# First token chunk of a fused attention and squared-ReLU MLP: who writes the high part of the squared features

## The chip, the cores and the metric

One core of one Trainium2 chip runs the whole program. The metric is the device time of one execution in microseconds (us). Three executions of the kernel before took 881.85, 885.22 and 885.75 us; their median is 885.22 us.

## What is computed

```
scores = q @ k.T / 8, masked by head: heads 0-3 see the last 32 positions,
         heads 4-7 see the positions of equal remainder mod 32
attn   = softmax(scores) @ v                      # 8 batches, 8 heads, 576 x 64
x      = attn as 4608 tokens x 512
h      = max(x @ w_in, 0)                         # 4608 x 2048
out    = (h * h) @ w_out                          # 4608 x 512, float32
```

## The kernel before

The 4608 tokens are worked off in 12 chunks of 384 (`TC`). For each chunk the 2048 hidden features are 16 steps of 128. `up(c, j)` (L462) forms the pre-activations of step `j` in a PSUM bank `h`, 128 x 384: every float32 operand is held as a high part, rounded to a shorter format, and a low part, the rest, and a product is the three matmuls high x high, high x low and low x high, so `up` has 12 matmuls of 384 columns. The three banks for `h` are used in turn, so step `j + 3` can start only when the last reader of step `j` is done. The squared ReLU is then split the same way into `gh` (high) and `gl` (the rest), and `down(c, j)` (L489) multiplies them with the output weights, 9 matmuls of 512 columns into three PSUM banks `y`. `down` runs two steps behind `up`.

The first chunk (`c == 0`) differs from the others. While it runs, the 16 weight tiles are still being decoded and split, two halves per step: ScalarE scales the raw words (L154) and makes the low bits `z` in a PSUM bank (L166), VectorE joins them (L169), ScalarE rounds the high part `w` (L172), GpSimd subtracts for the low part (L173). From the fourth step on there is one bank for `z`, so the next `z` waits for L169 of the one before. In the same stretch the attention of chunk 1 is computed: local heads in `pe_pair` (scores L319, row minima L324, GpSimd shift L347, exponential L348, GpSimd scaling L353, transposes L359 copied out by L360, product with v L367, then high part `xlh` on ScalarE, L382, and rest `xll` on VectorE, L383), and strided heads in `strided` (GpSimd products L412 and L434, VectorE sums L413 and L435, a softmax in between, L418 to L425, high part `xsh` L445, rest `xsl` on GpSimd L446). GpSimd also splits the first operands of chunk 2's attention (`kx` L218, `qx` L220, `vx` L255).

For the squared ReLU the first chunk uses a spare buffer `p_t` in SBUF: ScalarE writes `r = relu(h)` there (L470), VectorE writes `max(h, 0) * r` back over the bank `h` (L471), ScalarE rounds it into `gh` (L475), and VectorE subtracts, `gl = h - gh` (L476). In the later chunks ScalarE does ReLU, square and rounding (L473 to L475). `last["gh"]` names the ScalarE instruction behind which the two weight halves of the step are placed.

A scheduler that estimates each engine's time line sets the order of instructions on every engine's queue from the program order, so a change to one operation moves others. Each queue is worked off in order.

The text of the change's functions:

Of the kernel before, what the change touches and what calls it, by code (L numbers as in the profile page):

```python
# [11 lines left out]
AF = mybir.ActivationFunctionType  # L12
ALU = mybir.AluOpType
# [36 lines left out]
def f32(ap):  # L50
    return ap.bitcast(F32)
# [35 lines left out]
def attn_moe(ctx: ExitStack, tc, qk_l, v_l, qk_d, v_d, qk_p, v_p, f_s, q_s, k_s, v_s, w_in, w_out, masks, eye, out):  # L87
    nc = tc.nc
# [13 lines left out]
    def psum(i, nm):  # L102

        return ps.tile([P, 512], F32, name=nm, tag=f"ps{i}")
# [17 lines left out]
    last = {}  # L122
# [329 lines left out]
    def up(c, j):  # L452
        x = xt[c]
        p, o = divmod(j, 2)
        ph = psum((c * NFT + j) % 3, f"h{c}_{j}")
        n = 0
        for kt in range(4):
            kind, kk = "ls"[kt // 2], kt % 2
            xh, xl = x[kind, "h"][:, kk, :], x[kind, "l"][:, kk, :]
            wsl = slice(kt * 256 + o * P, kt * 256 + (o + 1) * P)  # L460
            for w, xx in ((wi[p][0], xh), (wi[p][0], xl), (wi[p][1], xh)):
                done = nc.tensor.matmul(ph[:, :TC], w[:, wsl], xx, start=n == 0, stop=n == 11)  # L462
                n += 1
        gh = gpool.tile([P, TC], F32R, name=f"gh{c}_{j}", tag="gh")
        gl = gpool.tile([P, TC], F32R, name=f"gl{c}_{j}", tag="gl")
        g = ph[:, :TC]
        if c == 0:

            r = p_t[j % 2].rearrange("p w q -> p (w q)")
            nc.scalar.activation(r, g, AF.Relu)  # L470
            nc.vector.scalar_tensor_tensor(out=g, in0=g, scalar=0.0, in1=r, op0=ALU.max, op1=ALU.mult)  # L471
        else:
            nc.scalar.activation(g, g, AF.Relu)  # L473
            nc.scalar.activation(g, g, AF.Square)  # L474
        last["gh"] = nc.scalar.copy(gh, g)  # L475
        nc.vector.tensor_sub(gl, g, f32(gh))  # L476
        g_tiles[c, j] = gh, gl
        return done
# [152 lines left out]
    for s in range(NS + 2):  # L631
        c, j = divmod(s, NFT)
        if s < NFT:
            up(c, j)
            if s >= 2:
                last["pe"] = down(*divmod(s - 2, NFT))

        elif s % 2 == 0:
            before, between, rest = plan[j // 2]
            for part, slots, two in (up, (s, s + 1), before), (down, (s - 2, s - 1), between):  # L640
                take(c + 1, two)
                with tc.issue_after(last["pe"].ins):
                    for i in slots:
                        if 0 <= i < NS:
                            last["mm"] = part(*divmod(i, NFT))
                last["pe"] = last["mm"]
            take(c + 1, rest)
# [110 lines left out]
```

## Time and profile before

| what | value |
|---|---|
| time, median of three | 885.22 us (881.85 to 885.75) |
| the profiled execution's own time | 883.18 us |
| its span, first to last instruction | 881.4 us |
| TensorE busy | 868.5 us of the span |
| ScalarE instructions L470 and L475 in the first chunk | 16 each |
| VectorE instructions L471 and L476 in the first chunk | 16 each |

The page gives busy times for TensorE (PE; PEld are its weight loads), VectorE (DVE), ScalarE (ACT) and GpSimd (POOL). The first chunk's matmuls run from about 31 to 114 us of the span, those of chunk 1 begin at 105 us, and the two overlap there because `down` lags. Matmuls are pipelined: a row of x2 in 0.52 us means that the second began 0.17 us after the first.

### The profile page before, as it was taken

The numbers are of one execution on the slowest core, as the hardware profiler recorded it, in microseconds if no ns is written. First come the engines' busy times: TensorE is split into PE (matmuls) and PEld (weight loads), VectorE is DVE, ScalarE is ACT, GpSimd is POOL, SyncE is SP. The second block draws the span as 40 slices with busy tenths as digits, with TensorE's granted clock in tenths as the row PEclk, the third lists the DMA queues.
The fourth block names the chain that finished last, engine by engine and source line by source line (L and its number), as shares of the span: only waits on it lengthen the run. The fifth ranks groups of instructions, "written<-read, shape, count | busy, mean of one in ns | idle before, by whom it ended". The sixth has DMA issues, their size and how long they took to land.

```text
span 881.4 us, 14862 instructions
## 1 busy us (share of the span) xinstructions
PE 868.5 (99%) x4744; PEld 789.6 (90%) x4744; DVE 635.5 (72%) x1892; ACT 572.6 (65%) x1510; POOL 676.8 (77%) x722
## 2 busy tenths in 40 slices
PE   8899999999999999999999999999999999999997
PEld 7788899999999999999999999999999989998996
DVE  4578687788777888878778778778787787883111
ACT  6798776676676666757657747657666665664332
POOL 4698878878978989898988978997898899782000
PEclk9999999999999999999999999999999999999999
DMA  9851631323123123104102302312131121000000
GB/s 356 355 195 63 184 121 42 103 84 113 32 66 112 37 89 103 44 30 127 44 13 80 115 14 74 104 31 74 31 102 57 30 71 61 7 1 10 28 1 36
DMA packets 26798, 71.41 MB, mean 81 GB/s; under 512 B 2976, under 2 KB 8736, under 8 KB 25184
## 3 DMA queue, kind: packets, MB, share of 16 engines
q1 hardware_dynamic: 26432, 70.14, 23.9%
q8 instruction: 37, 0.61, 0.3%
q10 hardware_dynamic: 288, 0.33, 0.1%
q14 instruction: 41, 0.34, 0.1%
HBM read 61.01 MB, written 9.44 MB: 80 GB/s over the span
## 4 chain that ended last, share of the span: by engine, by line
PE 95%; ACT 3%; DVE 1%; POOL 0%; issue 0%; DVEq 0%; POOLq 0%; ACTq 0%
PE h L462 44%; PE y L489 44%; PE s L234 2%; PE o L280 2%; ACT e L345 1%; PE w_ps L586 1%; ACT raw L154 1%; PE b L319 1%; DVE sc L419 0%; ACT z L166 0%; ACT w L172 0%; DVE raw L169 0%; ACT pt L360 0%; PE b L359 0%; DVE xsl L383 0%
## 5 line engine op out<-in xcount | busy, mean ns | idle before, releaser
L489 PE MATMUL y<-w,gh 128*128 128x512 f32 x1152 | 357.1, 391 | 0.8 <-ACT gh L475 0.8
L489 PEld LDWEIGHTS y<-w,gh 128*128 128x128 f32 x1152 | 212.5, 188 | 41.5 <-ACT gh L475 1.4
L462 PE MATMUL h<-xlh,w 128*128 128x384 f32 x768 | 229.6, 339 | 2.1 <-DVE xsl L383 1.6
L462 PE MATMUL h<-xsh,w 128*128 128x384 f32 x768 | 226.2, 335 | 0.0
L489 PE MATMUL y<-w,gl 128*128 128x512 f32 x576 | 224.0, 392 | 0.0
L434 POOL TENSOR_TENSOR pp<-vs,sc 128x448 f32<-128x448 f32 (+10 forms) x192 | 189.8, 1014 | 39.8 <-DVE qs L435 18.2
L412 POOL TENSOR_TENSOR pq<-ks,qs 128x512 f32<-128x512 f32 (+2 forms) x192 | 197.8, 1050 | 17.9 <-DVE sc L413 13.8
L476 DVE TENSOR_TENSOR gl<-h,gh 128x384 fp32r<-128x384 f32 x192 | 105.4, 550 | 84.2 <-ACT gh L475 82.9
L475 ACT CAST gh<-h 128x384 fp32r<-128x384 f32 x192 | 91.4, 477 | 103.0 <-PE y L489 100.0
L473 ACT ACTIVATE h<-h 128x384 f32<-128x384 f32 x176 | 83.0, 472 | 107.8 <-PE h L462 106.2
L413 DVE TENSOR_REDUCE sc<-pq 128x8 f32<-128x512 f32 (+4 forms) x228 | 119.6, 534 | 46.2 <-POOL pq L412 43.9
L462 PEld LDWEIGHTS h<-xlh,w 128*128 128x128 f32 x768 | 142.1, 188 | 5.6 <-DVE xsl L383 1.8
L462 PEld LDWEIGHTS h<-xsh,w 128*128 128x128 f32 x768 | 141.7, 188 | 0.3
L462 PE MATMUL h<-xll,w 128*128 128x384 f32 x384 | 129.3, 337 | 0.0
L435 DVE TENSOR_REDUCE qs<-pp 128x64 f32<-128x448 f32 (+11 forms) x192 | 106.7, 563 | 31.0 <-POOL pp L434 29.5
L489 PEld LDWEIGHTS y<-w,gl 128*128 128x128 f32 x576 | 108.1, 188 | 22.9
L462 PE MATMUL h<-xsl,w 128*128 128x384 f32 x384 | 128.5, 335 | 0.0
L474 ACT ACTIVATE h<-h 128x384 f32<-128x384 f32 x176 | 83.2, 473 | 3.6
L259 DVE STREAM_TRANSPOSE p_t<-e 32x128 f32<-32x128 f32 x240 | 72.3, 301 | 10.4 <-ACT e L248 6.0
L462 PEld LDWEIGHTS h<-xll,w 128*128 128x128 f32 x384 | 72.5, 189 | 2.2
L462 PEld LDWEIGHTS h<-xsl,w 128*128 128x128 f32 x384 | 72.2, 188 | 0.0
L243 ACT ACTIVATE e<-e,nm 96x128 f32<-96x128 f32 x160 | 62.5, 392 | 10.5 <-DVE nm L226 8.8
(97 smaller groups left out, 1077.2 us busy)
## 6 DMA issues: line engine op xcount, KB each, us to landing
qk<-qk_l SPq DMA_DIRECT2D x24, 400.0 KB, 3.2
y<-ysb SPq DMA_DIRECT2D x36, 256.0 KB, 3.7
raw<-w_in SPq DMA_DIRECT2D x7, 1024.0 KB, 11.2
qk<-qk_l SPq DMA_DIRECT2D x16, 416.0 KB, 3.3
vs<-v_s SPq DMA_DIRECT2D x10, 576.0 KB, 4.0
raw<-w_out SPq DMA_DIRECT2D x5, 1024.0 KB, 12.9
v<-v_l SPq DMA_DIRECT2D x40, 128.0 KB, 2.0
ks<-k_s SPq DMA_DIRECT2D x8, 576.0 KB, 3.8
```

The costliest lines, as they stand in the source:

```text
L243: nc.scalar.activation(e[:QC, cut(w)], e[:QC, cut(w)], AF.Exp, bias=nmax[:QC, w : w + 1], scale=-1.0, accum_out=ssum[:QC, w, :1])
L259: nc.vector.transpose(out=pt[STR * k : STR * (k + 1), :, STR * r : STR * (r + 1)], in_=e.rearrange("p (w k) -> p w k", k=KW)[STR * r : STR ...
L412: nc.gpsimd.tensor_mul(pv, kt[:, a : a + m, :], qt[:, i - i0 : i - i0 + 1, :].broadcast_to([P, m, D]))
L413: nc.vector.tensor_reduce(out=sc[:, i - i0, a : a + m], in_=pv, op=ALU.add, axis=AX.X)
L434: nc.gpsimd.tensor_mul(pv, vt[:, a : a + nd, :n], sc[:, il : il + 1, :n].broadcast_to([P, nd, n]))
L435: nc.vector.tensor_reduce(out=ot[:, il, a : a + nd], in_=pv, op=ALU.add, axis=AX.X)
L462: done = nc.tensor.matmul(ph[:, :TC], w[:, wsl], xx, start=n == 0, stop=n == 11)
L473: nc.scalar.activation(g, g, AF.Relu)
L474: nc.scalar.activation(g, g, AF.Square)
L475: last["gh"] = nc.scalar.copy(gh, g)
L476: nc.vector.tensor_sub(gl, g, f32(gh))
L489: done = nc.tensor.matmul(y_ps[c][t], g[:, sl], w[:, wsl], start=j == 0 and k == 0, stop=j == NFT - 1 and k == 2)
```

## The change

In the first chunk the line with VectorE's multiplication becomes a loop that runs it twice on the same operands: once into `gh`, whose type does the rounding, and once over the bank `h`. The rounding on ScalarE stays for the later chunks alone. The diff also adds a second line with the ReLU of the first chunk: it writes the same values to the same buffer again, and it is now the one that `last["gh"]` names.

```diff
             r = p_t[j % 2].rearrange("p w q -> p (w q)")
             nc.scalar.activation(r, g, AF.Relu)
-            nc.vector.scalar_tensor_tensor(out=g, in0=g, scalar=0.0, in1=r, op0=ALU.max, op1=ALU.mult)
+            last["gh"] = nc.scalar.activation(r, g, AF.Relu)
+            for t in (gh, g):
+                nc.vector.scalar_tensor_tensor(out=t, in0=g, scalar=0.0, in1=r, op0=ALU.max, op1=ALU.mult)
         else:
             nc.scalar.activation(g, g, AF.Relu)
             nc.scalar.activation(g, g, AF.Square)
-        last["gh"] = nc.scalar.copy(gh, g)
+            last["gh"] = nc.scalar.copy(gh, g)
         nc.vector.tensor_sub(gl, g, f32(gh))
```

In the changed program the two ReLUs are L470 and L471, the multiplications L473, the subtraction L478, `down` L491.

**Where the order moves, first place.** VectorE at the first steps of the first chunk, before (L413 and L418 belong to the strided attention of batch 2, L169 to the weights):

```order
L413 TENSOR_REDUCE sc_2_694<-pq_2_1_0_699 128x2
L471 SCALAR_TENSOR_TENSOR h_0_531<-h_0_531,p_t_90 128x384
L413 TENSOR_REDUCE sc_2_694<-pq_2_2_0_702 128x3
L471 SCALAR_TENSOR_TENSOR h_1_562<-h_1_562,p_t_91 128x384
L413 TENSOR_REDUCE sc_2_694<-pq_2_3_0_705 128x4
L476 TENSOR_TENSOR gl_0_545<-h_0_531,gh_0_544 128x384
L169 SCALAR_TENSOR_TENSOR raw_267<-raw_267,z_0_551 128x512
```

and VectorE at the same place with the change:

```order
L413 TENSOR_REDUCE sc_2_698<-pq_2_1_0_703 128x2
L413 TENSOR_REDUCE sc_2_698<-pq_2_2_0_706 128x3
L473 SCALAR_TENSOR_TENSOR gh_0_544<-h_0_531,p_t_90 128x384
L473 SCALAR_TENSOR_TENSOR h_0_531<-h_0_531,p_t_90 128x384
L413 TENSOR_REDUCE sc_2_698<-pq_2_3_0_709 128x4
L169 SCALAR_TENSOR_TENSOR raw_267<-raw_267,z_0_552 128x512
L413 TENSOR_REDUCE sc_2_698<-pq_2_4_0_712 128x5
L478 TENSOR_TENSOR gl_0_545<-h_0_531,gh_0_544 128x384
```

One more reduction now stands ahead of the first multiplication, and the subtraction for `gl_0` has the second multiplication, two reductions and a weight join between it and `gh_0`.

**Second place.** TensorE where the first chunk hands over to chunk 1, before (`h_0` and `h_1` are steps 0 and 1 of chunk 1, `y` with `gl_13` is the end of `down` of step 13):

```order
L489 MATMUL y_2_614<-w_6_1218,gl_13_1307 128x512
L462 MATMUL h_0_1397<-xlh_901,w_0_413 128x384
L462 MATMUL h_0_1397<-xll_902,w_0_413 128x384
L462 MATMUL h_0_1397<-xlh_901,w_0_413 128x384 x2
L462 MATMUL h_0_1397<-xll_902,w_0_413 128x384
L462 MATMUL h_0_1397<-xlh_901,w_0_413 128x384
```

and with the change:

```order
L491 MATMUL y_2_617<-w_6_1230,gl_13_1320 128x512
L462 MATMUL h_0_1413<-xlh_908,w_0_413 128x384
L462 MATMUL h_0_1413<-xll_909,w_0_413 128x384
L462 MATMUL h_0_1413<-xlh_908,w_0_413 128x384
L462 MATMUL h_1_1432<-xlh_908,w_0_413 128x384
L462 MATMUL h_1_1432<-xll_909,w_0_413 128x384
L462 MATMUL h_1_1432<-xlh_908,w_0_413 128x384
L367 MATMUL b_1_1_1295<-pt_1_1_693,v_1_1_690 64x96 x8
L462 MATMUL h_0_1413<-xlh_908,w_0_413 128x384
L462 MATMUL h_1_1432<-xlh_908,w_0_413 128x384
L462 MATMUL h_0_1413<-xll_909,w_0_413 128x384
L462 MATMUL h_0_1413<-xlh_908,w_0_413 128x384
```

The product with v for the second pair of local heads (L367), which stood inside step 14 before, now stands inside the first steps of chunk 1, and the matmuls that follow read what is made from it.

**Third place.** ScalarE at the same hand-over with the change, from the ReLU of step 15 to the first operation of chunk 1 (before, L382 of the second pair stood ahead of the ReLU of step 14, with 11 instructions between it and the first operation of chunk 1):

```order
L470 ACTIVATE p_t_91<-h_15_1382 128x384
L166 ACTIVATE z_512_1290<-raw_512_1109 128x512
L172 CAST w_7_1284<-raw_0_1107 128x512
L217 CAST kx_0_1377<-qk_0_1366 128x448
L219 CAST qx_0_1376<-qk_0_1366 128x384
L254 CAST vx_0_1618<-v_0_1367 128x4x64
L471 ACTIVATE p_t_91<-h_15_1382 128x384
L445 CAST xsh_910<-qkvs_3_981 128x2x192
L172 CAST w_7_1284<-raw_512_1109 128x512
L360 COPY pt_1_1_693<-b_1_1_1249 128x384
L382 CAST xlh_908<-b_1_1_1295 128x384
L475 ACTIVATE h_0_1413<-h_0_1413 128x384
```

The copy L360 that the product waits for, and the rounding L382 behind it, are now the last ScalarE work of the first chunk. On GpSimd the rest `xsl` (L446) moves in the same way, from ahead of `kx`, `qx`, `vx` to behind them:

```order
L173 TENSOR_TENSOR w_7_1284<-raw_0_1107,w_7_1284 128x512
L404 MEMSET sc_4_1510 128x108
L412 TENSOR_TENSOR pq_4_0_0_1512<-qkvs_4_1508 128x64
L412 TENSOR_TENSOR pq_4_1_0_1515<-qkvs_4_1508 128x128
L218 TENSOR_TENSOR kx_0_1377<-qk_0_1366,kx_0_1377 128x448
L220 TENSOR_TENSOR qx_0_1376<-qk_0_1366,qx_0_1376 64x384
L255 TENSOR_TENSOR vx_0_1618<-v_0_1367,vx_0_1618 128x4x64
L662 MEMSET p_t_90 128x384
L446 TENSOR_TENSOR xsl_911<-qkvs_3_981,xsh_910 128x2x192
```

Before, L446 stood right ahead of the first of these rows.

## Rows read from the trace of the kernel before

**Rows 1.** Busy time by stretch (us:us, length, engines with instruction counts, granted clock, DMA).
```profile
core 0: us, PE busy (x) PEld busy (x) DVE busy (x) ACT busy (x) POOL busy (x), PEclk, DMA share, GB/s
36.00:106.00 70.00, 68.73 (x381) 59.82 (x380) 53.70 (x139) 61.50 (x116) 60.57 (x66) 1.00 0.44 155
106.00:200.00 94.00, 93.99 (x496) 85.83 (x495) 73.61 (x246) 64.72 (x187) 76.27 (x91) 1.00 0.30 92
200.00:876.00 676.00, 676.00 (x3535) 617.62 (x3534) 490.13 (x1419) 420.15 (x1141) 522.79 (x541) 1.00 0.18 56
```

**Rows 2.** TensorE in order of time (start us, us, count, idle before) at its two waits.
```profile
39.17 1.66 PE L489 MATMUL y<-w,gh 128*128 128x512 f32 x6 [0.79 <-ACT gh L475]
40.66 0.62 PE L489 MATMUL y<-w,gl 128*128 128x512 f32 x2
...
89.56 0.44 PE L462 MATMUL h<-xlh,w 128*128 128x384 f32 x1 [0.48 <-DVE gl L476]
89.84 0.34 PE L462 MATMUL h<-xll,w 128*128 128x384 f32 x1
90.02 0.51 PE L462 MATMUL h<-xlh,w 128*128 128x384 f32 x2
```

**Rows 3.** VectorE groups from 36 to 106 us (busy us, mean ns, idle before).
```profile
L169 DVE SCALAR_TENSOR_TENSOR raw<-raw,z 128x512 uint32<-128x512 uint32 x26 | 17.8, 683 | 5.0 <-ACT z L166 4.6
L471 DVE SCALAR_TENSOR_TENSOR h<-h,p_t 128x384 f32<-128x384 f32 x16 | 9.0, 561 | 4.6 <-ACT p_t L470 4.5
L476 DVE TENSOR_TENSOR gl<-h,gh 128x384 fp32r<-128x384 f32 x14 | 7.6, 551 | 1.7 <-ACT gh L475 1.7
```

**Rows 4.** ScalarE groups from 36 to 106 us.
```profile
L470 ACT ACTIVATE p_t<-h 128x384 f32<-128x384 f32 x16 | 7.7, 492 | 1.8 <-PE h L462 1.8
L475 ACT CAST gh<-h 128x384 fp32r<-128x384 f32 x14 | 6.8, 488 | 2.5 <-DVE h L471 1.8 <-PE y L489 0.6 <-DVE sm L424 0.2
L360 ACT COPY pt<-b 128x384 f32<-128x384 f32 x4 | 1.9, 482 | 0.4 <-PE b L359 0.4
L382 ACT CAST xlh<-b 128x384 fp32r<-128x384 f32 x2 | 1.0, 480 | 0.0
```

**Rows 5.** GpSimd, VectorE and ScalarE in order of time at the first step.
```profile
37.34 1.02 POOL L412 TENSOR_TENSOR pq<-qkvs 128x128 f32<-128x128 f32 x2
...
38.04 0.56 DVE L471 SCALAR_TENSOR_TENSOR h<-h,p_t 128x384 f32<-128x384 f32 x1
38.51 0.34 DVE L413 TENSOR_REDUCE sc<-pq 128x3 f32<-128x192 f32 x1
...
38.63 0.48 ACT L475 CAST gh<-h 128x384 fp32r<-128x384 f32 x1 [1.78 <-DVE h L471]
```

**Rows 6.** GpSimd, then VectorE, around 80 us in order of time.
```profile
79.16 5.15 POOL L173 TENSOR_TENSOR w<-raw,w 128x512 fp32r<-128x512 f32 x4
...
80.47 3.89 DVE L419 TENSOR_TENSOR sc<-sc,mx 128x36 f32<-128x36 f32 x1
```

**Rows 7.** ScalarE, GpSimd, VectorE, TensorE at the hand-over in order of time.
```profile
102.25 0.54 ACT L445 CAST xsh<-qkvs 128x384 fp32r<-128x384 f32 x1
...
105.73 0.67 ACT L172 CAST w<-raw 128x512 fp32r<-128x512 f32 x1
...
102.86 1.02 POOL L446 TENSOR_TENSOR xsl<-qkvs,xsh 128x384 fp32r<-128x384 f32 x1
103.98 1.31 POOL L173 TENSOR_TENSOR w<-raw,w 128x512 fp32r<-128x512 f32 x1
...
108.88 0.73 POOL L255 TENSOR_TENSOR vx<-v,vx 128x256 fp32r<-128x256 f32 x1
...
102.41 0.56 DVE L383 TENSOR_TENSOR xll<-b,xlh 128x384 fp32r<-128x384 f32 x1 [0.84 <-ACT xlh L382]
...
105.14 0.33 PE L462 MATMUL h<-xlh,w 128*128 128x384 f32 x1
110.09 0.62 PE L489 MATMUL y<-w,gh 128*128 128x512 f32 x2
```

**Rows 8.** All instructions of L169: least, median and greatest duration in ns.
```profile
L169 DVE SCALAR_TENSOR_TENSOR raw<-raw,z x32: 671/689/697, 18.6 to 103.4; 128x512 uint32<-128x512 uint32 x32
```

## The prediction

> **What bounds the kernel now.** I read busy time by stretch first. From 106 us to the end TensorE is busy without a hole, 93.99 of 94 us and 676 of 676, while VectorE, ScalarE and GpSimd stay at 81% or under [rows 1]. There an engine that waits costs nothing; only what ends the first chunk earlier or later moves the end. In the first chunk, 36 to 106 us, TensorE is busy 68.73 of 70 us, ScalarE 61.5, VectorE 53.7, GpSimd 60.6 [rows 1]. So I went on to TensorE's own time line there: it waits twice, 0.79 us for the first `gh`, and 0.48 us for a `gl` [rows 2], by the queue's order that of step 10, whose bank step 13 takes over. These 1.27 us are about all that the first chunk can give back, 0.14% of the time. What it can take has no such ceiling, because ScalarE and VectorE work there close behind TensorE.
>
> **What the change does to each engine.** ScalarE: 16 roundings of 0.488 us go, and 16 repeated ReLUs of 0.492 us come [rows 4], so its load stays where it was, +0.1 us. What it loses is a wait: a rounding had to wait for VectorE's product, 1.8 us in all, and all of it once, at the first step [rows 4, 5]; the repeated ReLU needs only what the first one needed. VectorE: the product into SBUF is new to the trace. Its nearest rows are the product into the bank, 0.561 us, and the subtraction into SBUF in the same rounded type, 0.551 us [rows 3]; I take 0.55, the row with the same output, and the larger weight join, 512 columns from PSUM and SBUF into SBUF at 0.683, bounds it from above [rows 3]. Sixteen are 8.8 us, at most 10.9. VectorE's 53.7 busy us become 62.5 of 70, 89%. Its 16.3 idle us cover that as long as they shrink with it: most are waits for ScalarE's `z` and ReLU, 4.6 and 4.5 us [rows 3]. What it costs if that cover is gone is the first rival. GpSimd and the DMA queues get nothing new; GpSimd's order changes at the hand-over (term 3).
>
> **The chain of one step.** Before: ReLU, product, rounding (`gh`), subtraction (`gl`). Now: two ReLUs, product (`gh`), product, subtraction (`gl`). `gh` has three operations as before, 0.49 + 0.49 + 0.55 against 0.49 + 0.56 + 0.49 [rows 3, 4]; `gl` has five instead of four and comes half a us later. In the steady part `down` runs two steps behind `up`, and a step is 12 matmuls at 0.17 us (0.51 for two, 0.34 for one [rows 2]) and 9 at 0.23 (0.62 for two [rows 7]), 4.1 us. So I cost that half us at nothing in steps 1 to 13. It shows at the first step and in what surrounds the last.
>
> **Term 1, the first step.** VectorE's queue is in order, and the third reduction now stands ahead of the product. Its operand was ready at 38.36, the end of GpSimd's second of two [rows 5]; the reduction takes 0.34, and an operation starts some 0.09 before the end of the one ahead (38.04 + 0.56 against 38.51 [rows 5]). So the product starts near 38.65 and `gh` is there at 39.2, where the rounding gave it at 39.11 [rows 5]: +0.1 us. Then `gl_0`: the second product, two reductions of about 0.4 and 0.5 and a weight join stand before it, from start to start 0.47, 0.33, 0.60 and 0.40, so that the subtraction starts at 40.9 and ends at 41.5. TensorE reaches its first `gl` matmul 1.5 us behind its first `gh` matmul [rows 2], at 40.75, so it stands 0.8 us. **Term 1 is +0.9 us**; 0 if the join doesn't hold it up, 1.5 if the join itself waits for its `z`.
>
> **Term 2, the wait at 89.56.** It comes from one VectorE operation: a subtraction of the strided softmax, 128 x 36 elements, stands 3.89 us, from 80.47 to 84.36, beside an unbroken run of four GpSimd subtractions that ends at 84.31 [rows 6]; all that is queued behind it was late, `gl` of step 10 too. With the change it stands behind `gl` of step 11. I take the wait as gone, **-0.6 us** with the slow start of the matmul behind it (0.44 for 0.34 us [rows 2]). Whether the stall then hits another step is a rival.
>
> **Term 3, the hand-over to chunk 1.** Before, `xll` and `xsl` were ready at 103.0 and 103.9 us, over a us ahead of chunk 1's first matmul at 105.14 [rows 7]. Now L360 and L382 end ScalarE's first chunk. From the end of step 15's matmuls ScalarE has nine operations and L360. The same nine (rounding `xsh`, `z`, two roundings of weights, `kx`, `qx`, `vx`, two ReLUs) ran in one piece from 102.25 to 106.40 [rows 7], 4.15 us, and L360 adds 0.4 [rows 4]: 4.55 us. TensorE has in that time 15 `down` matmuls at 0.23 and six of chunk 1 at 0.17, 4.5 us. So L367 just starts in time. But L382, 0.48 [rows 4], and L383, 0.56 [rows 7], now lie between it and what TensorE needs next, with two matmuls, 0.35 us, in between: about 0.8 us with the hand-offs. GpSimd is later still. Behind step 15, ReLU, `z` and a rounding take some 1.6 us until it may subtract; that subtraction to the end of `vx` took 103.98 to 109.61 [rows 7], 5.6 us, and `xsl` now follows with 1.02: 8.2 us. TensorE wants `xsl` after the 4.5 us, L367, eight more matmuls, 1.4 us, and the 0.8: near 7.1. I take **+1.6 us**, nearer to GpSimd's 1.9 than to the 0.8. Bounds: 0, if ScalarE and GpSimd run as far ahead as ScalarE does at the first step, and 4, if they are two to three us behind.
>
> **The sum.** +0.9 - 0.6 + 1.6 = +1.9 us on the profiled execution's 883.18: 885.1. That execution lies 2.0 us under the median of 885.22, and I set the change against the median: 887.1 us. About 0.5%, 4.4 us, is what a measurement of this kernel can tell from no change; the three runs themselves span 3.9 us. So I forecast no change that counts.
>
> **Rivals.** *VectorE becomes the pace of the first chunk.* Its waits are for ScalarE, whose next `z` waits for VectorE's last join: if the two hold each other, none of the 16.3 idle us shrinks and the 8.8 us come on top. The low part of the last weights' first half was ready at 105.29 and first wanted at 110.09 [rows 7], so 4.8 us are free, and TensorE stands for the other 4.0: 885.22 + 1.9 + 4.0 = 891.1, slower. It decides from the point where the last joins, the last at 103.4 before [rows 8], come more than 5 us later. Against it: 89% is not full, and ScalarE's 1.8 us head start. Chance 0.2.
>
> *The stalled subtraction hits harder.* Between `gl` of step 11 and `gh` of step 12 it holds up weight joins too. If its 3.9 us return where TensorE has some 2 us of slack, that is +2 us: 889.1. The row has a small operation wait out the rest of a run of four [rows 6]. The Trainium skill ("SBUF — State Buffer", Who interferes with whom) has a VectorE instruction with two SBUF inputs and a GpSimd one that reads SBUF exclude each other for one whole instruction; by that it would wait for one GpSimd subtraction, 1.3 us, and this rival would cost nothing. The measured stall speaks for the longer price. The new products have one operand in PSUM, as the joins do, and no join took over 0.697 us [rows 8], so the products themselves aren't held. Chance 0.12.
>
> *ScalarE's freedom carries through.* Weights and attention run 1.8 us ahead from the first step on, the hand-over is covered and both waits go: 885.22 - 1.3 = 883.9. It can't give 0.5%. Chance 0.18.
>
> *The change doesn't do what it says.* ScalarE's rounding goes, but the repeated ReLU takes its slot, so only the wait is freed; this is in the sum already.
>
> **Chances and range.** The forecast has 0.5. Low end: the third rival less the runs' scatter, 883.0; high end: the first rival, 891.1, say 891.5. Over 4.4 us slower is reached by most of the first rival and a little of the second: 0.18. No mechanism gives over 4.4 us faster; scatter leaves 0.04. The rest, 0.78, is within 0.5%.
>
> **What would show it.** Right: no wait of TensorE after 115 us; at 40 us one of 0.8 us, now ahead of the first `gl`; none near 89; one to two us in all between L367 and the first `xsl` matmuls near 107; VectorE at 62 busy us in the first chunk, the new products at 0.55. Wrong: a first chunk longer by over 4 us with weights (L172, L173) as releaser, or products into `gh` far from 0.55.

## The result, and the profile after

The changed kernel took 885.94 us, the median of 20 runs (884.58 to 887.51), beside 884.47 us for the kernel before on the same chips (881.85 to 886.27). The ratio is 1.0019, with a 95% interval of 1.0012 to 1.0026: slower by 1.5 us, within the 0.5% that the prediction called no change, and 1.2 us under its 887.1 us. The changed kernel's profiled execution took 886.62 us, its span 884.8 us.

One thing is needed to compare profiles. Each run's record gives its mean granted clock, and the runs here fall in two groups, 0.993 to 0.998 and 0.985 to 0.990; three executions that fall in neither are left out below, one of the kernel before (0.947, 883.44 us), one of x1 (3251 us) and one of w1 (1742 us). The first views show where the second group loses. Busy time by stretch of the profiled execution of the kernel before (columns as in [rows 1]), from 16 to 36 us, while attention and weights are being prepared:

```profile
16.00:28.00 12.00, 8.25 (x109) 5.98 (x109) 6.35 (x22) 9.64 (x22) 8.27 (x10) 1.00 1.01 416
28.00:36.00 8.00, 6.39 (x44) 6.17 (x39) 4.18 (x7) 7.27 (x13) 4.27 (x4) 0.79 1.02 411
```

The same view of the changed kernel, and its first chunk and the rest:

```profile
16.00:28.00 12.00, 10.42 (x85) 8.07 (x86) 6.34 (x21) 8.43 (x18) 7.55 (x9) 0.60 1.02 420
28.00:36.00 8.00, 7.56 (x51) 6.61 (x50) 3.65 (x6) 7.21 (x12) 3.40 (x3) 0.54 1.01 407
36.00:106.00 70.00, 68.59 (x371) 60.25 (x370) 59.69 (x153) 62.78 (x118) 60.14 (x65) 1.00 0.44 152
106.00:200.00 94.00, 92.88 (x499) 84.32 (x498) 71.70 (x240) 63.18 (x181) 74.76 (x90) 1.00 0.31 94
200.00:876.00 676.00, 676.00 (x3538) 617.79 (x3537) 492.67 (x1427) 422.32 (x1147) 525.95 (x544) 1.00 0.18 56
```

Here TensorE was at its lower level (1.2 GHz) for most of 16 to 36 us, in the profiled execution before only briefly behind 28 us. The two programs have the same TensorE work in that stretch, and yet the last `up` matmul ahead of the first `down` began at 38.04 us before and at 39.82 us after. So 1.8 of the 3.4 us between the two spans lie ahead of the change, 1.45 between there and the last matmul, and 0.2 behind it. Of the 89 runs of the kernel before in these groups, 34 were in the lower one, and on the mean 1.8 us longer (885.12 against 883.35 us). Compared group with group, the change costs **+2.0 us** (11 runs at the higher clock, 885.36 us) and **+1.8 us** (9 runs at the lower, 886.88 us). The forecast was +1.9. The 89 runs come from the four chips of the experiments; against runs of their own chip alone, the versions in the table below move by up to 0.3 us in the higher group and 0.7 in the lower. For the 20 runs of the kernel before beside the changed kernel there are no clocks.

From 200 us on nothing changed, TensorE is busy without a hole as in [rows 1]. From 106 to 200 us it lost 1.1 us. Its time line in the changed kernel, at the five places where it starts late (idle before in brackets):

```profile
40.99 1.66 PE L491 MATMUL y<-w,gh 128*128 128x512 f32 x6 [0.83 <-DVE gh L473]
43.23 0.97 PE L491 MATMUL y<-w,gl 128*128 128x512 f32 x3 [0.58 <-DVE gl L478]
...
107.38 0.88 PE L367 MATMUL b<-pt,v 128*64 128x96 f32 x16 [0.31 <-ACT pt L360]
108.84 0.62 PE L462 MATMUL h<-xlh,w 128*128 128x384 f32 x2 [0.58 <-ACT xlh L382]
...
110.98 0.44 PE L462 MATMUL h<-xsl,w 128*128 128x384 f32 x1 [0.23 <-POOL xsl L446]
```

The first row was there before as 0.79 us [rows 2]; the wait near 89 us of [rows 2] is gone; the other four are new. The bracket is less than what is lost, because the matmul behind a hole starts up slowly. Counted from start to start, and less the usual step, they are 1.00, 0.75, 0.48, 0.77 and 0.40 us, 3.4 us in all; before, 0.95 and 0.66, 1.6 us in all. That is 1.8 us more; from the 38.04 (39.82) matmul to the last matmul of the program it took 1.45 us longer. The 0.35 us between the two counts are not explained.

### The profile page after: what moved, and what is told of

Its sections match the earlier page's. It is cut to its first block, busy times and chain, and to the rows that moved or that the text cites. A ratio compares the mean times of both kernels' runs of the same rounds, so it can differ in the third digit from the quotient of the medians.

```text
span 884.8 us, 14867 instructions
## 1 busy us (share of the span) xinstructions
PE 873.3 (99%) x4744; PEld 793.2 (90%) x4744; DVE 642.2 (73%) x1908; ACT 573.7 (65%) x1510; POOL 677.2 (77%) x722
## 4 chain that ended last, share of the span: by engine, by line
PE 93%; DMA 2%; ACT 2%; POOL 2%; DVE 1%; issue 0%; DVEq 0%; SPq 0%; POOLq 0%; ACTq 0%
PE h L462 44%; PE y L491 43%; PE s L234 2%; PE o L280 2%; DMA raw<-w_in 1%; POOL w L173 1%; ACT raw L154 1%; DMA qk<-qk_d 1%; DMA raw<-w_out 1%; PE b L319 0%; ACT w L172 0%; PE b L359 0%; ACT z L166 0%; PE b L378 0%; PE b L367 0%
## 5 line engine op out<-in xcount | busy, mean ns | idle before, releaser
L491 PE MATMUL y<-w,gh 128*128 128x512 f32 x1152 | 356.7, 391 | 0.8 <-DVE gh L473 0.8
L491 PEld LDWEIGHTS y<-w,gh 128*128 128x128 f32 x1152 | 212.5, 188 | 40.9 <-DVE gh L473 1.1
L491 PE MATMUL y<-w,gl 128*128 128x512 f32 x576 | 224.0, 392 | 0.6 <-DVE gl L478 0.6
L478 DVE TENSOR_TENSOR gl<-h,gh 128x384 fp32r<-128x384 f32 x192 | 105.4, 549 | 83.1 <-ACT gh L477 81.7
L413 DVE TENSOR_REDUCE sc<-pq 128x8 f32<-128x512 f32 (+4 forms) x228 | 119.4, 533 | 46.2 <-POOL pq L412 43.6
L477 ACT CAST gh<-h 128x384 fp32r<-128x384 f32 x176 | 83.7, 476 | 104.3 <-PE y L491 103.3
L491 PEld LDWEIGHTS y<-w,gl 128*128 128x128 f32 x576 | 107.9, 188 | 23.9 <-DVE gl L478 1.0
```

The costliest lines, as they stand in the source:

```text
L413: nc.vector.tensor_reduce(out=sc[:, i - i0, a : a + m], in_=pv, op=ALU.add, axis=AX.X)
L491: done = nc.tensor.matmul(y_ps[c][t], g[:, sl], w[:, wsl], start=j == 0 and k == 0, stop=j == NFT - 1 and k == 2)
```

## The experiments

The order theory says that TensorE pays at few places, where the instruction it needs stands late in another engine's queue. Its rivals: VectorE's 16 more products cost by themselves; the repeated ReLU, which keeps ScalarE as full as before, costs; the stalled subtraction L419 decides. All times in the table are against the kernel before. "At like clock" is the difference of the means in the higher and the lower group, with the number of runs. The waits are those of TensorE in each kernel's profiled execution, counted from start to start as above (only those over 0.2 us): in the 12 us from the first step on, from there to 100 us, and behind 100 us. "To the end" is the time from the last `up` matmul ahead of the first `down` to the last matmul, less that of before. "Stall" is the second L419 on VectorE. In x2, y3, z2 and z3 the clock fell a second time, inside the first chunk, so that their groups do not tell the start alone.

| kernel | ratio (95%) | at like clock, us | waits first, middle, hand-over | sum | to the end | stall, us |
|---|---|---|---|---|---|---|
| before | | 0 | 0.95, 0.66, 0 | 1.6 | 0 | 3.89 |
| changed | 1.0019 (1.0012 to 1.0026) | +2.0 (11), +1.8 (9) | 1.75, 0, 1.64 | 3.4 | +1.45 | 0.18 |
| x1 | 0.9998 (0.9988 to 1.0008) | +0.3 (9), -0.4 (2) | 1.80, 0, 1.02 | 2.8 | +0.92 | 1.59 |
| x2 | 1.0044 (1.0028 to 1.0060) | +3.9 (2), +3.5 (4) | 0.97, 3.62, 0 | 4.6 | +3.78 | 4.71 |
| x3 | 1.0032 (1.0021 to 1.0043) | +3.3 (7), +2.7 (5) | 1.89, 1.53, 0 | 3.4 | +1.88 | 4.60 |
| x4 | 1.0020 (1.0008 to 1.0032) | +1.9 (5), +1.5 (7) | 1.37, 1.81, 0.47 | 3.7 | +1.98 | 3.68 |
| y1 | 1.0009 (0.9999 to 1.0019) | +1.3 (10), +0.9 (1) | 1.27, 0, 2.17 | 3.4 | +1.45 | on GpSimd |
| y2 | 1.0011 (0.9999 to 1.0024) | +1.1 (6), +1.1 (6) | 0.94, 0, 1.70 | 2.6 | +1.01 | 0.19 |
| y3 | 1.0049 (1.0031 to 1.0068) | +4.8 (5), +5.4 (1) | 1.03, 0, 4.38 | 5.4 | +5.48 | on GpSimd |
| y4 | 1.0022 (1.0009 to 1.0035) | +2.1 (8), +2.0 (4) | 1.42, 0, 2.37 | 3.8 | +1.67 | on GpSimd |
| z1 | 1.0007 (0.9998 to 1.0016) | +0.9 (7), +0.4 (4) | 1.10, 0.87, 0 | 2.0 | +0.48 | 3.16 |
| z2 | 1.0036 (1.0023 to 1.0048) | +3.5 (3), +2.7 (2) | 0.83, 2.94, 0 | 3.8 | +2.97 | 6.03 |
| z3 | 1.0086 (1.0071 to 1.0101) | +7.6 (1), +6.3 (4) | 0, 4.16, 1.15 | 5.3 | +5.36 | 4.47 |
| w1 | 1.0008 (0.9998 to 1.0018) | -0.2 (4), -0.2 (7) | 1.13, 0, 0.74 | 1.9 | +0.08 | on GpSimd |

**x1: the hand-over undone, the rest left.** Issuing the strided attention of chunk 1 sooner moves L367 of the second pair into step 15 and the second `xsl` ahead of `kx`.

```diff
-SPREAD = ((11, 8), (13, 13))
+SPREAD = ((11, 6), (13, 13))
```

> The change whole, and one dial besides: the strided attention of chunk 1 is issued over six steps instead of eight, which puts L367, L382 and the second xsl (L446) back inside step 15 of the first chunk. The first step keeps the order of the change. Order theory (TensorE pays at two places of the queues): the first-step wait for gl stays at 0.6 to 0.8 us, the three waits near 107 to 110 us (0.48 + 0.77 + 0.40 = 1.6) go; time 1.6 under the changed kernel, so 0 +-0.8 us against before. If the stalled subtraction L419, now ahead of gl of step 10 again, brings the wait near 89 back, 0.6 more. VectorE-load theory (the 16 more products cost whatever the order): as the changed kernel, +1.5 against before. Repeated-ReLU theory (ScalarE held full): also +1.5.

It took what the kernel before takes, 1.7 us less than the changed kernel at the higher clock and 2.1 at the lower, with all 16 products and all 16 repeats in it. That fits the order theory and neither load theory. The trace shows only a part of it: in the profiled execution, which at 884.16 us lies 0.5 us above the mean of its group, the waits at the hand-over are 0.6 us less than in the changed kernel, and the time to the end 0.5 us less. Of the three hand-over waits two are gone; the one for `xlh` came again, larger:

```profile
106.65 0.69 PE L462 MATMUL h<-xlh,w 128*128 128x384 f32 x2 [0.85 <-ACT xlh L382]
```

**z2: the control, the same dial on the kernel before.**

> The kernel before with nothing but the dial of x1: the strided attention of chunk 1 over six steps instead of eight. It is the control of x1. If the dial repairs what the change did to the hand-over, it has nothing to repair here: 0 +-0.6 against before. If the dial is worth 1.6 by itself, whatever the chain, the time is 1 to 1.6 under before and x1 says nothing of the change. If the earlier strided work meets a long run of GpSimd (L419 over 3.5 us), 1 to 2 more than before.

The third case came, and more of it: +3.5 and +2.7 us. The dial gains nothing by itself, and x1's gain is not simply the dial's. What it would be worth here without the stall is not known, because it sent the softmax of the strided attention into a long run of GpSimd. GpSimd, VectorE, then TensorE, each in order of time:

```profile
73.35 2.61 POOL L173 TENSOR_TENSOR w<-raw,w 128x512 fp32r<-128x512 f32 x2
75.90 2.06 POOL L353 TENSOR_TENSOR e<-e,rs 96x512 f32<-96x512 f32 x2
77.89 1.06 POOL L347 TENSOR_TENSOR e<-e,nm 96x512 f32<-96x512 f32 x1
78.89 1.31 POOL L173 TENSOR_TENSOR w<-raw,w 128x512 fp32r<-128x512 f32 x1
...
74.23 6.03 DVE L419 TENSOR_TENSOR sc<-sc,mx 128x36 f32<-128x36 f32 x1
...
81.84 0.45 PE L462 MATMUL h<-xlh,w 128*128 128x384 f32 x1 [2.77 <-DVE gl L476]
```

**x2: the old chain at steps 0 and 1.** It gives VectorE's first step back the order of before.

```diff
+            if j <= 1:
+                nc.vector.scalar_tensor_tensor(out=g, in0=g, scalar=0.0, in1=r, op0=ALU.max, op1=ALU.mult)
+                last["gh"] = nc.scalar.copy(gh, g)
+            else:
```

> The old chain (one product, ScalarE's rounding) at steps 0 and 1, the new chain at steps 2 to 15. On VectorE's queue the first step is as before the change, and the hand-over has L367 at step 11 and the second xsl ahead of kx. Order theory: both places are undone; no wait ahead of the first gl beyond 0.1 us, no waits near 107 to 110; what stays is the saving of the wait at 89, if it stays: between -0.7 and 0.3 us against before. VectorE-load theory: 14 of 16 products are still there, so +1.3. Repeated-ReLU theory: 14 of 16 repeats still there, +1.3.

A miss: +3.9 us where -0.7 to +0.3 was expected. Both places of the order theory are undone, as it said (0.97 us at the first step, nothing behind 100 us). A third place opened. VectorE, ScalarE (idle while it waits for L419) and TensorE, from 82 to 93 us:

```profile
82.90 4.71 DVE L419 TENSOR_TENSOR sc<-sc,mx 128x36 f32<-128x36 f32 x1
...
87.65 0.23 ACT L420 ACTIVATE sc<-sc 128x36 f32<-128x36 f32 x1 [3.24 <-DVE sc L419]
...
92.49 0.98 PE L495 MATMUL y<-w,gh 128*128 128x512 f32 x3 [2.07 <-ACT w L172]
```

and busy time by stretch behind that wait:

```profile
92.00:93.00 1.00, 0.51 (x2) 0.47 (x3) 1.00 (x3) 1.00 (x3) 0.49 (x1) 1.00 0.00 0
93.00:94.00 1.00, 1.00 (x5) 0.90 (x5) 1.00 (x3) 1.00 (x3) 0.84 (x1) 0.73 0.00 0
94.00:95.00 1.00, 1.00 (x7) 0.91 (x6) 1.00 (x3) 0.59 (x2) 0.60 (x1) 0.50 0.41 57
```

The stall cost the wait and then some 3 us at half clock. So the prediction's second rival is a real mechanism; it did not strike in the changed kernel.

**x3: the new chain at step 0 alone.** The mirror of x2: VectorE has one product more instead of 16 (`if j > 0` takes the old chain).

> The new chain at step 0 alone, the old one at steps 1 to 15. VectorE gets one product more (0.55 us) instead of 16, ScalarE one repeat. On VectorE's queue the first step has the order of the change, with the product of step 1 also ahead of gh of step 0; the hand-over has L367 between the first matmuls of chunk 1, L382 last on ScalarE and the second xsl behind vx, as with the change. Order theory: the waits of the change without its load: gh 0.5 to 1 more, gl 0.6 to 0.8, hand-over 1 to 2, so +1.5 to +3 against before. VectorE-load theory: +0.1. Repeated-ReLU theory: +0.1.

At like clock it is 1.3 and 0.9 us slower than the changed kernel, with a sixteenth of its added load on VectorE. So neither load theory can be the whole cause. The order theory has the size and the first step (waits of 0.97 us for `gh` and 0.59 us for `gl`), but not the place of the rest: at the hand-over all was in time, and a wait of 1.37 us for a `gl` at 91.97 us, behind an L419 of 4.60 us, took its place. TensorE at the first step, then VectorE, then TensorE:

```profile
41.21 1.66 PE L495 MATMUL y<-w,gh 128*128 128x512 f32 x6 [0.97 <-DVE gh L477]
43.45 0.96 PE L495 MATMUL y<-w,gl 128*128 128x512 f32 x3 [0.59 <-DVE gl L482]
...
86.38 4.60 DVE L419 TENSOR_TENSOR sc<-sc,mx 128x36 f32<-128x36 f32 x1
...
91.97 0.44 PE L462 MATMUL h<-xlh,w 128*128 128x384 f32 x1 [1.37 <-DVE gl L482]
```

**x4: VectorE's load alone, in the old chain.** The extra product goes into `gl`, which the subtraction overwrites.

```diff
-            nc.vector.scalar_tensor_tensor(out=g, in0=g, scalar=0.0, in1=r, op0=ALU.max, op1=ALU.mult)
+            for t in (gl, g):
+                nc.vector.scalar_tensor_tensor(out=t, in0=g, scalar=0.0, in1=r, op0=ALU.max, op1=ALU.mult)
```

> The chain of before with one VectorE product more per step, written into gl, where the subtraction overwrites it (its value is never used). VectorE carries the whole load of the change and more (old queue, 16 x 0.55 = 8.8 us), ScalarE's rounding stays and waits for the second product. The hand-over keeps the order of before. Order theory: only the first step pays: gh 0.55 later, gl not much more; +0.3 to +1.0 against before, no waits near 107. VectorE-load theory: at least the +1.5 of the change, 2 to 4 us if the products take the place of VectorE's waits one for one.

+1.9 and +1.5 us: more than the order theory said, at the lower end of the load theory. Its waits are 1.20 us at the first step, where the product now delays the rounding, 0.72 and 0.77 us at 90 and 92 us, behind an L419 of 3.68 us, and 0.31 us at 111 us.

**y4 and y1: the stall taken out of x4 and x2.** L419 of chunk 1 runs on GpSimd:

```diff
-            nc.vector.tensor_sub(s, s, mx[:, :ni].unsqueeze(2).broadcast_to([P, ni, i1]))
+            (nc.gpsimd if c == 1 else nc.vector).tensor_sub(s, s, mx[:, :ni].unsqueeze(2).broadcast_to([P, ni, i1]))
```

> The kernel of x2 (old chain at steps 0 and 1, new chain at 2 to 15) with L419 of chunk 1, the 128 x 36 subtraction of the strided softmax, on GpSimd instead of VectorE. In x2 it stood 4.71 us on VectorE beside a run of GpSimd operations, TensorE waited 2.07 us near 90 us, and the granted clock was 0.50 for some 3 us after. Stall theory (that operation, wherever it lands, is what moves the first chunk): on GpSimd it takes under 0.5 us, the wait near 90 and the slow stretch go, and the time is 3 to 4 us under x2, -0.7 to +0.6 against before. VectorE-load theory: 14 more products stay, at most 0.5 us less than x2, +3 against before.

> The kernel of x4 (old chain and one unused VectorE product per step into gl, overwritten by the subtraction) with L419 of chunk 1 on GpSimd. VectorE keeps all 16 more products; x4 measured +1.7 at like granted clock, with L419 standing 3.68 us and two waits of 0.9 near 90. Stall theory: those two waits go, the first gh wait of 1.2 stays, +0.2 to +0.8 against before. VectorE-load theory: +1.5 stays.

On GpSimd the subtraction takes 0.24 to 0.26 us, and in both kernels the waits near 90 us are gone. With the 3.24 us that ScalarE stood for L419 in x2, that points to the stall as their cause; it does not isolate it, because the order moved again, and 2.2 and 2.4 us of waits came at the hand-over. For y1 that leaves +1.3 where at most +0.6 was expected (2.5 less than x2), for y4 nothing gained at all.

**y2: the repeated ReLU out.**

```diff
-            nc.scalar.activation(r, g, AF.Relu)
             last["gh"] = nc.scalar.activation(r, g, AF.Relu)
```

> The change without the repeated ReLU: ScalarE does one ReLU per step of the first chunk, 16 x 0.49 = 7.9 us less than the changed kernel. The hand-over keeps the order of the change (L367 between the first matmuls of chunk 1, second xsl behind vx). Order and stall theory: the first-step waits stay (gh 0.8 to 1.0, gl 0.6 to 0.8), at the hand-over ScalarE's L360 and L382 may come sooner (up to 1.2 us less), xsl stays late; +0.5 to +1.8 against before, and up to 2 more where L419 stands beside a long run of GpSimd. Repeated-ReLU theory (ScalarE held full takes the gain away): at least 1.8 under the changed kernel, 0 or less against before.

+1.1 us in both groups: the repeat costs 0.7 to 0.9 of the change's 1.8 to 2.0, and not the whole. By the waits nearly all of it is at the first step, where they were expected to stay and fell from 1.75 to 0.94 us. VectorE's queue there has two reductions ahead of the product where the changed kernel has three, `gh` is there at 39.16, and TensorE starts on it at 39.21 us with a lag of 0.32 us instead of 1.00. VectorE, then TensorE in y2:

```profile
38.41 0.29 DVE L413 TENSOR_REDUCE sc<-pq 128x2 f32<-128x128 f32 x1 [0.20 <-POOL pq L412]
38.61 0.55 DVE L472 SCALAR_TENSOR_TENSOR gh<-h,p_t 128x384 fp32r<-128x384 f32 x1
...
39.21 1.66 PE L490 MATMUL y<-w,gh 128*128 128x512 f32 x6
41.33 0.98 PE L490 MATMUL y<-w,gl 128*128 128x512 f32 x3 [0.45 <-DVE gl L477]
```

**z1 and w1: what x1 and y2 each took away, together; w1 with L419 on GpSimd too.**

> The change without the repeated ReLU and with the strided attention of chunk 1 issued over six steps instead of eight: the two edits that each took most of the loss away, together. Order theory with the first step as y2 showed it (without the repeat the first gh comes 0.68 us sooner) and the hand-over as x1 showed it (second xsl in time, 0.85 us for xlh left): x1's +0.2 less 0.7, so -0.5 against before, between -1.2 and +0.3. Rival (the waits only move: what is taken away at one place comes back at another, because ScalarE, VectorE and GpSimd together are behind by then): +0.5 to +1.5, with the waits of TensorE from 36 to 120 us again at 2 us or more in sum.

> The kernel of z1 (no repeated ReLU, strided attention of chunk 1 over six steps) with L419 of chunk 1 on GpSimd. Here the order of the first step and of the hand-over stays that of z1, so that L419's engine is all that changes there. In z1 L419 stood 3.16 us on VectorE, and TensorE waited 0.57 and 0.29 us at 86 and 96 us for weights that came late behind it; its waits in the first chunk were 1.97 us in sum, against 1.61 before. Stall theory: both go, the sum falls to 1.1 to 1.3, the time 0.3 to 1.0 under z1 and 0 to 0.7 under before: the first version under both kernels. Rival (what is taken away at one place comes back at the hand-over, as in y1 and y4, where 2.2 and 2.4 us came there): a new wait behind 104 us, +0.5 to +1.5 against before.

z1 kept y2's first step and had no wait at the hand-over, but behind an L419 of 3.16 us there were 0.87 us of waits near 86 and 96 us: +0.9 and +0.4, where -1.2 to +0.3 was expected. In w1 these are gone, and 0.74 us came at 108.54 us for `xll`. At -0.2 us in both groups (+0.1 against the runs of its own chip) w1 is level with the kernel before and 2 us under the changed one. No version here beat the kernel before.

**z3 and y3: two more that lost.** z3 has the old chain at step 0 alone (`if j == 0`), y3 is y1 with x1's dial.

> The old chain at step 0 alone, the change at steps 1 to 15, so that the first step has one product and ScalarE's rounding. Order theory: first gh wait as before (0.9), gl wait 0 to 0.3 instead of 0.7; L367 of the second pair stands at the start of step 14, so the three hand-over waits of the change should be under 0.5 in sum, and the rest hangs on L419: with it under 1.5 us, -0.6 to +0.6 against before; with it over 3.5 us, a wait of 0.7 to 2.2 near 90 us and +1 to +3.5. VectorE-load theory: +1.4 with no wait above 1 us anywhere.

> The kernel of y1 with the strided attention of chunk 1 issued over six steps instead of eight: the old order at the first step, L419 of chunk 1 on GpSimd, L367 of the second pair inside step 15 and the second xsl ahead of kx, qx, vx. Order and stall theory: only the first gh wait of 0.8 is left, so the lowest time of all, -0.3 to -1.0 against before. VectorE-load theory: +1.3 or more.

z3 had the first step in time and the largest loss of all, +6.3 and +7.6 us where at most +3.5 was expected: L419 stood 4.47 us and TensorE waited 2.61 and 0.90 us behind it. y3 was to be the best and lost 4.8 us in another way. No L419 stood on VectorE, though an L425 of the same softmax stood 2.38 us at 82.69 us. The last piece of the output weights came late: its transfer was issued at 98.8 us (95.7 before; 1.8 us of the 3.1 are the later start) and landed 6.3 us after that (5.1 before). What made the issue later than the start does is open. ScalarE, then TensorE:

```profile
105.46 0.67 ACT L154 ACTIVATE raw<-raw 128x512 f32<-128x512 f32 x1 [2.44 <-DMA raw<-w_out]
...
112.26 0.69 PE L462 MATMUL h<-xlh,w 128*128 128x384 f32 x1 [3.90 <-DVE gl L482]
```

**Read together.** The column "to the end" follows the sum of waits. In the nine kernels whose clock stayed up in the first chunk (all but x2, y3, z2 and z3), the loss there differs from the waits added to the 1.6 us of before by at most 0.5 us; in those four a wait of over 2 us was followed by half clock, and they lost 0.8 to 1.7 us beyond the waits. So in the profiled executions whose clock held, TensorE's waits in the first chunk account for the loss to within half a us. Against the means at like clock one execution is not enough: x1 (0.92 against +0.3 and -0.4), x3 (1.88 against +3.3 and +2.7) and z3 (5.36 against +7.6 and +6.3) differ by 0.6 to 2.2 us. Which waits there are is set by the order on the queues, and every edit here moved several at once.

## Why the prediction was right

**The bound and the sum.** From 116 us on TensorE's queue gave nothing and took nothing; the three waits of the hand-over lie between 107 and 111 us, inside the stretch that the prediction called without a hole in the kernel before. No version gave back the 1.27 us, which are 1.6 when counted from start to start. +1.9 was forecast, +2.0 and +1.8 came at like clock and +1.5 between the medians; by the waits the three terms are +0.8, -0.7 and +1.6. Of the 1.2 us by which 887.1 was too high, 0.75 is the base, 885.22 as the median of three against 884.47 of twenty. The half us of `gl` that was put at nothing in steps 1 to 13 cost nothing: no wait between 43.23 and 107.38 us.

**Term 1, +0.9: right in size and mechanism.** Measured: `gh` 0.04 us later by TensorE's lag (+0.1 said), `gl` 0.75 (0.8 said). VectorE's queue did it, as the order had said:

```profile
40.11 0.35 DVE L413 TENSOR_REDUCE sc<-pq 128x3 f32<-128x192 f32 x1 [0.28 <-POOL pq L412]
40.38 0.55 DVE L473 SCALAR_TENSOR_TENSOR gh<-h,p_t 128x384 fp32r<-128x384 f32 x1
40.85 0.56 DVE L473 SCALAR_TENSOR_TENSOR h<-h,p_t 128x384 f32<-128x384 f32 x1
41.31 0.41 DVE L413 TENSOR_REDUCE sc<-pq 128x4 f32<-128x256 f32 x1
41.64 0.68 DVE L169 SCALAR_TENSOR_TENSOR raw<-raw,z 128x512 uint32<-128x512 uint32 x1
42.23 0.48 DVE L413 TENSOR_REDUCE sc<-pq 128x5 f32<-128x320 f32 x1
42.63 0.54 DVE L478 TENSOR_TENSOR gl<-h,gh 128x384 fp32r<-128x384 f32 x1
```

What the prediction missed is how cheap it was to avoid: without the repeat the third reduction stands behind the product (y2), worth 0.7 us of TensorE's lag.

**Term 2, -0.6: right in size, with luck.** The wait of 0.66 us is gone. In the changed kernel the second L419 came at 90.92 us, where GpSimd had just ended one operation and began the next, and took 0.18 us; it was another small operation of the softmax that then stood, without TensorE waiting for it:

```profile
90.92 0.18 DVE L419 TENSOR_TENSOR sc<-sc,mx 128x36 f32<-128x36 f32 x1
92.62 2.96 DVE L423 TENSOR_SCALAR sm<-sm 128x6 f32<-128x6 f32 x1
```

That the stall was gone, and not only moved to where it costs nothing, was luck: the second rival, given 0.12, did not strike here, but it did in x2, x3, x4, z2 and z3.

**Term 3, +1.6: right in size, its split off.** The three hand-over waits are 0.48, 0.77 and 0.40 us, 1.64 in all. The prediction had L367 start in time, 0.8 for L382 and L383, and the rest of 1.6 for GpSimd's `xsl`. The wait behind L382 is 0.77 as said, but L367 waited too, 0.48, and `xsl` cost 0.40 and not 0.8. That the two errors cancel is luck: ScalarE, at 108.30, and GpSimd, at 109.91, in order of time:

```profile
106.83 0.50 ACT L360 COPY pt<-b 128x384 f32<-128x384 f32 x1
108.30 0.48 ACT L382 CAST xlh<-b 128x384 fp32r<-128x384 f32 x1 [0.98 <-PE b L367]
...
109.91 1.01 POOL L446 TENSOR_TENSOR xsl<-qkvs,xsh 128x384 fp32r<-128x384 f32 x1
```

x1, back at the time before with the same load, speaks for the order there and not the load, though its trace shows only 0.6 us less of waits at the hand-over. How much the load would have cost in the order of before is open: x4 and y4, at +1.5 to +2.1, carry it in chains and orders of their own.

**The load.** VectorE's busy time from 36 to 106 us went from 53.70 to 59.69, +6.0 and not +8.8. The products have the duration that was said, 0.549 us each, but the prediction counted durations where the engine's time goes by starts: an operation starts some 0.09 us before the end of the one ahead, which it had used in term 1 and not here. From 40.38 to 40.85 us above, a product takes 0.47 us of VectorE. The stretch holds 30 products where it held 16 [rows 3], since those of the last step fell behind 106 us, and 14 at 0.47 us are 6.6 us; an L383 fell behind 106 us too.

```profile
L473 DVE SCALAR_TENSOR_TENSOR h<-h,p_t 128x384 f32<-128x384 f32 x15 | 8.3, 553 | 0.0
L473 DVE SCALAR_TENSOR_TENSOR gh<-h,p_t 128x384 fp32r<-128x384 f32 x15 | 8.2, 549 | 3.5 <-PE y L491 3.3 <-ACT z L166 0.2
L478 DVE TENSOR_TENSOR gl<-h,gh 128x384 fp32r<-128x384 f32 x15 | 8.2, 544 | 0.1
```

The first rival, VectorE as the pace of the chunk, did not come: at 85% of 70 us it still had idle time, and the last join started at 103.8 us against 103.4. The third rival, ScalarE's freedom, did not come either, and y2, which frees ScalarE of 16 operations more, was still 1.1 us over the kernel before.

## What to carry to other kernels

Where TensorE is full but for a few named waits, forecast a change by where it moves the instructions that those waits hang on, and look at the queue order of every engine around them before counting load. A change of one operation in a scheduled kernel is never one change: of twelve edits here, most opened a wait at a place that the edit did not touch, so a version is judged by all its waits, not by the one that it was made to remove. And compare executions at like granted clock when the effect is 2 us, since the start alone can differ by 1.8.

## What the runs showed of the hardware that was not expected

- **A small VectorE operation between SBUF operands can wait out a whole run of GpSimd.** The subtraction of 128 x 36 elements took 0.18 us where it was not held. It stood 3.89, 1.59, 4.71, 4.60, 3.68, 3.16, 6.03 and 4.47 us in eight kernels, and in each it ended within 0.1 us of the end of GpSimd's unbroken run; in z2 that run was the rest of one operation and five more. The Trainium skill ("SBUF — State Buffer", Who interferes with whom) has the one hold the other off for one whole instruction, here 1.3 us; the runs show several in a row. L423, which adds a constant to 128 x 6 elements, stood up to 2.96 us in the same way. The products, with an operand in PSUM, did not: the 15 into `gh` between 36 and 106 us took 542 to 557 ns in the changed kernel.
- **Four long waits of TensorE went with half clock.** With TensorE's waits of 2.07 (x2), 2.77 (z2), 2.61 (z3) and 3.90 us (y3) the granted clock fell to 0.50 for some microseconds, in y3 while TensorE still stood; with the wait of 1.37 us in x3 it stayed at 1.00. In y3:

```profile
110.00:112.00 2.00, 0.00 (x0) 0.00 (x0) 2.00 (x6) 1.35 (x4) 1.90 (x2) 0.71 0.89 265
112.00:113.00 1.00, 0.74 (x2) 0.74 (x3) 0.67 (x2) 0.00 (x0) 0.95 (x2) 0.50 0.32 57
113.00:114.00 1.00, 1.00 (x4) 1.00 (x4) 0.35 (x1) 0.00 (x0) 1.00 (x2) 0.50 0.75 180
```

- **The start has several courses.** With 347 matmuls recorded ahead of it in every program, the last `up` matmul ahead of the first `down` began at 38.0 to 38.1 us in five profiled executions and at 39.5 to 39.9 us in seven, with the clock at half for most of 16 to 36 us in the seven; y2 (38.73) and z3 (39.21) lie between. By the mean clock, 34 of 89 runs of the kernel before and 9 of 20 of the changed one took the longer course. What chooses is open.
